# Loading w_in in 2 KB runs from the second chunk on, in a fused attention and feed-forward kernel

## The chip, the cores and the metric

The kernel runs on one core of a Trainium2 chip. The metric is device time in microseconds (us), from one launch to its end; where several runs are given, the median counts. The engines are named as the profile names them: PE is the matrix engine (PEld its weight loads), DVE the vector engine, ACT the scalar engine, POOL the GpSimd engine, and SP the engine that issues most of the transfers (DMA).

## The reference

```
# q, k, v: (8 batches, 8 heads, 576, 64) float32
kv  = einsum('bhsd,bhse->bhde', k, v)
out = einsum('bhsd,bhde->bhse', q, kv)
rms = sqrt(mean(out*out, axis=-1) + 1e-6)
x   = (out / rms * g_norm) -> reshaped to (4608 tokens, 512)

h = x @ w_in               # w_in:  512 x 2048
g = maximum(0.01*h, h)
y = g @ w_out              # w_out: 2048 x 512, y float32
```

The set-up scales the two weight matrices by a float64 number, so they reach the kernel as 8-byte floats and the kernel rounds them to 4-byte floats itself. One row of w_in is 2048 x 8 B = 16 KB, so 128 neighbouring columns of one row are a run of 1 KB, and 256 are a run of 2 KB.

## The kernel before

The 4608 tokens go through in 9 blocks of 512. The first block's feed-forward is done with plain products while the weights are still arriving; the later blocks use a Strassen scheme (seven products in place of eight), in the third and later blocks nested once more for the first product. Only the first block meets the weight loads, so the parts below are those.

w_in is held as four chunks `c`, each of two halves `h` (left and right half of the 2048 columns), each of two parts `u` of 128 columns. A part has four slices `e` of 128 rows.

```python
P, NE, U, NC = 128, 4, 2, 4
NW = U * NE * P
# all of w_in in one tile; per chunk and half the order is part, slice, column
w1_sb = [[view(w1_all, (2 * c + h) * NW, U, NE, P) for c in range(NC)] for h in range(2)]
w2_sb = [[consts.tile([P, U, DM], F32, ...) for c in range(NC)] for h in range(2)]

# seven landing places of 4 KB per partition, used in turn
raw_homes = itertools.cycle([view(stage, i * NW, NW) for i in range(3)]
                            + [pair(i, NW) for i in range(4)])

def load(t, src, eng):          # w_in: 4 transfers, of 32 partitions each; w_out: 1 transfer
    ...
def round_f64(dst, raw):
    lo, hi = raw[:, :, 0], raw[:, :, 1]
    add = spare(...);  pin(nc.scalar.activation(add, lo, func=AF.Copy, scale=2.0 ** -29))
    cut = spare(...);  pin(nc.scalar.activation(cut, hi, func=AF.Copy, scale=2.0 ** -112))
    yield
    pin(nc.vector.tensor_scalar(cut, cut, HIGH_MOST, -HIGH_MOST, ...))       # L246
    yield
    pin(nc.vector.tensor_scalar(dst, cut, 3, None, op0=logical_shift_left))  # L250
    yield
    pin(nc.vector.scalar_tensor_tensor(dst, in0=cut, ..., in1=dst, ...))     # L252
    yield
    pin(nc.vector.tensor_tensor(dst, dst, add, op=ALU.add))                  # L255

w_in_e = w_in.rearrange("(p t i) f -> p i t f", p=NP, i=E)
w_jobs = []
for c in range(NC):
    for h in range(2):
        for u in range(U):
            f0 = h * (DF // 2) + (c * U + u) * P
            w_jobs += [(w1_sb[h][c][:, u], w_in_e[:, :, :, f0:f0 + P]),
                       (w2_sb[h][c][:, u:u + 1, :], w_out[f0:f0 + P].unsqueeze(1))]
w_jobs[1:-1] = [...]     # neighbours swapped: w_in 0, w_in 1, w_out 0, w_in 2, w_out 1, ...
```

There are so 32 jobs of 512 KB, 16 of w_in and 16 of w_out, each a load and a rounding (two operations of ACT, four of DVE). Jobs 0 to 6 are loaded during the attention of the first batch. The first block's loop then runs over the 16 parts n; `between` loads and rounds more jobs ahead of need:

```python
for n in range(2 * NC * U + 1):
    if n < 2 * NC * U:
        c, h, u = n // (2 * U), n // U % 2, n % U
        for e in range(NE):       # product "h_ps" of part n, needs w_in part n
            matmul(h_ps[:, cols], lhsT=w1_sb[h][c][:, u, e, :], rhs=x[:, e, cols], ...)
        act = nc.scalar.activation(gT, h_ps, func=AF.Prelu, alpha=SLOPE)
    ...
    for t in range(4):            # product "o_acc" of part n - 1, needs w_out part n - 1
        matmul(accs[t], lhsT=now[0][:, t * P:(t + 1) * P], rhs=now[1], ...)
    between(n, 1)

def between(n, half):             # cut
    while half and rounded < min(3 * n + 8, 2 * n + 13, len(w_jobs) - (n < 11)):
        if loaded < len(w_jobs):
            load_w(loaded); loaded += 1
            if loaded in (15, 19):
                load_pair(1, (loaded - 15) // 4)     # k, v, q of the second batch
        round_w(rounded); rounded += 1
```

After the first block, w_in in SBUF is read by additions (`sides_w1` on POOL, `combine` on POOL and DVE) and by transfers to a DRAM copy that later blocks read back; all of these index it as `[:, u, e, column]`.

Of the kernel before, what the change touches and what calls it, by code (L numbers as in the profile page):

```python
# [23 lines left out]
def kernel(  # L24
# [38 lines left out]
    DM, DF = w_in.shape  # L63
    P = 128
    NE = DM // P
# [7 lines left out]
    U = 2  # L73
    NC = DF // 2 // (U * P)
# [24 lines left out]
    NW = U * NE * P  # L99
    w1_all = consts.tile([P, 2 * NC * NW], F32, name="w1_all")  # L100
# [4 lines left out]
    def view(t, lo, *shape):  # L105
        n = 1
        for d in shape:
            n *= d
        t = t[:, lo:lo + n]
        names = "abcd"[:len(shape)]  # L110
        return t.rearrange(f"p ({' '.join(names)}) -> p {' '.join(names)}",
                           **dict(zip(names, shape))) if len(shape) > 1 else t
# [83 lines left out]

    w1_sb = [[view(w1_all, (2 * c + h) * NW, U, NE, P) for c in range(NC)] for h in range(2)]
    w2_sb = [[consts.tile([P, U, DM], F32, name=f"w2_{h}_{c}") for c in range(NC)]  # L200
             for h in range(2)]

# [53 lines left out]

    w_in_e = w_in.rearrange("(p t i) f -> p i t f", p=NP, i=E)
    w_jobs = []
    for c in range(NC):
        for h in range(2):  # L260
            for u in range(U):
                f0 = h * (DF // 2) + (c * U + u) * P
                w_jobs += [(w1_sb[h][c][:, u], w_in_e[:, :, :, f0:f0 + P]),
                           (w2_sb[h][c][:, u:u + 1, :], w_out[f0:f0 + P].unsqueeze(1))]

    w_jobs[1:-1] = [w_jobs[i + 1 if i % 2 else i - 1] for i in range(1, len(w_jobs) - 1)]
    w_raws = {}

    def load_w(j, *eng):
# [700 lines left out]
    x_sides, _, sums, _ = sides_x(1)  # L970
# [128 lines left out]
```

## Time and profile before

| | before |
|---|---|
| device time, median of 3 runs | 927.6 us (926.85 to 929.41) |
| span of the profiled run | 925.5 us |
| PE busy | 915.1 us, 99% of the span |
| DVE, ACT, POOL busy | 615.5, 328.7, 317.6 us |
| DMA packets, bytes | 90066, 200.03 MB |

The profile gives the busy time of each engine, then a strip of the span in 40 equal slices, then the transfers, then the chain of work that ended last, then the groups of instructions. A busy PE is the product itself; an idle time is listed under the engine that waited, with what it waited for. A group row ends with how long the engine stood idle ahead of the group and what released it. Two rows of the page say how long an operation of DVE takes on a contiguous tile and on one with a stride between its four rows of 128 elements (`g` is laid out so):

```profile
L610 DVE TENSOR_TENSOR o<-o_c,o 128x512 f32<-128x512 f32 x104 | 71.6, 688 | 117.8 <-PE o_c L118 117.6
...
L610 DVE TENSOR_TENSOR g<-g,pairs 128x512 f32<-128x512 f32 x84 | 55.6, 689 | 1.9
```

### The profile page before, as it was taken

Reading aid. Unit: us, or ns where it says so; the run is one execution under the profiler, and the core shown is the slowest. Engines: PE = TensorE matmul, PEld = TensorE weight load, DVE = VectorE, ACT = ScalarE, POOL = GpSimd, SP = SyncE. Lnnn points to the kernel's source line nnn. Section 1 sums busy time; section 2 is a strip of 40 time slices with the busy share of each in tenths; the row PEclk is TensorE's granted clock in tenths of the full one; section 3 lists DMA queues with packets and bytes.
Section 4 is the critical chain, followed back from the end, with each engine's and each line's share of the span. In section 5 each row is a group of like instructions: output and inputs, shape, how many; then the busy total and the mean of one; then the engine's idle time right before and its main releaser. Section 6 shows DMA issues by size and latency. Waiting matters only on the chain.

```text
span 925.5 us, 17566 instructions
## 1 busy us (share of the span) xinstructions
PE 915.1 (99%) x6856; PEld 776.5 (84%) x6856; DVE 615.5 (67%) x998; ACT 328.7 (36%) x651; POOL 317.6 (34%) x318
## 2 busy tenths in 40 slices
PE   8999999999999999999999999999999999999998
PEld 5544447888998999899999999999988999999996
DVE  4866995587456876597757875687558744654454
ACT  4544532242135233532343423342333333223330
POOL 2000354967622542236211711272225322532222
PEclk9999999999999999999999999999999999999999
DMA  9999936895598678856995599668755676667632
GB/s 270 223 234 217 238 114 193 276 301 165 150 348 266 185 208 297 274 174 189 280 297 181 173 282 276 219 183 229 252 174 175 197 220 186 185 196 220 187 121 91
DMA packets 90066, 200.03 MB, mean 216 GB/s; under 512 B 9856, under 2 KB 42112, under 8 KB 89984
## 3 DMA queue, kind: packets, MB, share of 16 engines
q1 hardware_dynamic: 79392, 186.85, 68.9%
q10 hardware_dynamic: 10144, 10.88, 3.4%
q8 instruction: 55, 0.90, 0.4%
q0 software_dynamic: 448, 1.18, 0.3%
q14 instruction: 27, 0.22, 0.1%
HBM read 172.39 MB, written 26.48 MB: 215 GB/s over the span
## 4 chain that ended last, share of the span: by engine, by line
PE 95%; DMA 2%; DVE 2%; issue 0%; ACT 0%; POOL 0%; SPq 0%; ACTq 0%; DVEq 0%; POOLq 0%
PE o_a L118 21%; PE o_c L118 21%; PE h_ha L118 11%; PE h_hb L118 8%; PE h_hc L118 8%; PE h_hd L118 6%; PE o_acc L118 6%; PE h_ps L118 6%; PE o_ps L118 2%; PE kv_ps L118 2%; PE h_a L118 1%; PE h_b L118 1%; DMA pairs<-in_v_dram 1%; PE h_c L118 1%; PE h_d L118 1%; DMA pairs<-in_moe_w_in_dram 1%
## 5 line engine op out<-in xcount | busy, mean ns | idle before, releaser
L610 POOL TENSOR_TENSOR gs<-g 128x512 f32<-128x512 f32 x64 | 80.8, 1282 | 442.3 <-ACT g L781 442.3
L610 DVE TENSOR_TENSOR o<-o_c,o 128x512 f32<-128x512 f32 x104 | 71.6, 688 | 117.8 <-PE o_c L118 117.6
L781 ACT ACTIVATE g<-g 128x512 f32<-128x512 f32 x124 | 78.2, 631 | 123.4 <-DVE g L610 123.4
L845 ACT COPY w_all<-h_ha 128x512 f32<-128x512 f32 x84 | 48.7, 580 | 186.6 <-PE h_ha L118 186.6
L610 DVE TENSOR_TENSOR o<-o_a,o 128x512 f32<-128x512 f32 x88 | 60.4, 687 | 63.4 <-PE o_a L118 63.3
L118 PE MATMUL o_c<-pairs,gs 128*128 128x256 f32 x384 | 91.3, 381 | 0.0
L118 PE MATMUL o_a<-pairs,gs 128*128 128x256 f32 x384 | 90.8, 379 | 0.0
L118 PEld LDWEIGHTS o_c<-pairs,gs 128*128 128x128 f32 x384 | 69.8, 190 | 9.3 <-issue 1.4
L118 PEld LDWEIGHTS o_a<-pairs,gs 128*128 128x128 f32 x384 | 69.8, 190 | 7.8
L118 PE MATMUL o_c<-w,g 128*128 128x256 f32 x256 | 61.6, 383 | 0.0
L118 PE MATMUL o_a<-w,g 128*128 128x256 f32 x256 | 61.5, 383 | 0.0
L118 PEld LDWEIGHTS h_ha<-stage,w_all 128*128 128x128 f32 x448 | 58.7, 192 | 2.8
L118 PE MATMUL h_ha<-stage,w_all 128*128 128x128 f32 x448 | 59.0, 275 | 0.0
L118 PE MATMUL h_ps<-xT,w_all 128*128 128x512 f32 (+1 forms) x136 | 57.9, 570 | 0.2 <-DVE w_all L255 0.2
L118 PE MATMUL o_acc<-w,g 128*128 128x512 f32 x128 | 57.8, 595 | 0.0
L610 DVE TENSOR_TENSOR g<-g,pairs 128x512 f32<-128x512 f32 x84 | 55.6, 689 | 1.9
L118 PEld LDWEIGHTS o_a<-w,g 128*128 128x128 f32 x256 | 46.4, 190 | 11.0 <-ACT pairs L845 3.1
L610 POOL TENSOR_TENSOR pairs<-w_all 128x512 f32<-128x512 f32 x8 | 11.5, 1438 | 123.5 <-DMA stage<-in_moe_w_in_dram 95.1
L118 PEld LDWEIGHTS o_c<-w,g 128*128 128x128 f32 x256 | 46.4, 190 | 5.8
L118 PEld LDWEIGHTS h_ps<-xT,w_all 128*128 128x128 f32 x136 | 25.5, 190 | 29.2 <-issue 26.5
L118 PEld LDWEIGHTS o_acc<-w,g 128*128 128x128 f32 x128 | 24.0, 190 | 29.8 <-issue 29.4
L610 DVE TENSOR_TENSOR w_all<-h_hc,w_all 128x512 f32<-128x512 f32 x56 | 38.4, 686 | 15.6 <-PE h_hc L118 15.4
(196 smaller groups left out, 2028.0 us busy)
## 6 DMA issues: line engine op xcount, KB each, us to landing
w_all<-w SPq DMA_DIRECT2D x196, 448.0 KB, 4.3
pairs<-w SPq DMA_DIRECT2D x56, 512.0 KB, 4.5
out_dram<-o ACTq DMA_DIRECT2D x36, 256.0 KB, 4.5
v_in<-in_v_dram SPq DMA_DIRECT2D x29, 288.0 KB, 5.7
k_in<-in_k_dram SPq DMA_DIRECT2D x28, 288.0 KB, 6.3
q_in<-in_q_dram SPq DMA_DIRECT2D x56, 144.0 KB, 6.6
q_in<-in_q_dram SPq DMA_DIRECT2D x56, 140.0 KB, 6.6
w<-stage SPq DMA_DIRECT2D x12, 512.0 KB, 4.6
```

The costliest lines, as they stand in the source:

```text
L118: pin(nc.tensor.matmul(*args, **kw))
L610: ins = eng.tensor_tensor(out_, a, b_, op=ALU.subtract if minus else ALU.add)
L781: nc.scalar.activation(t, t if src is None else src, func=AF.Prelu, alpha=SLOPE)
L845: nc.scalar.copy(q[:, at], banks[tag])
```

## The change

From the second chunk on, a job of w_in no longer is one part of 128 columns with all four slices. It is half of the slices (two) for both parts together, 256 neighbouring columns, so that each run in DRAM is 2 KB long where it was 1 KB. It is meant to let the transfers of w_in run with half as many, longer pieces. To make room for that, the order in SBUF becomes slice, part, column; and since both jobs of a half chunk are now needed for either of its parts, the list of jobs is sorted anew: both w_in jobs of a half chunk stand at the place of the first, and the w_out jobs follow. The first chunk keeps its jobs and its order of jobs, but its destination in SBUF gets a stride (four rows of 128, with 256 between their starts).

```diff
-    w1_sb = [[view(w1_all, (2 * c + h) * NW, U, NE, P) for c in range(NC)] for h in range(2)]
+    w1_sb = [[view(w1_all, (2 * c + h) * NW, NE, U, P).rearrange("p e u m -> p u e m")
+              for c in range(NC)] for h in range(2)]
 ...
-    for c in range(NC):
-        for h in range(2):
-            for u in range(U):
-                f0 = h * (DF // 2) + (c * U + u) * P
-                w_jobs += [(w1_sb[h][c][:, u], w_in_e[:, :, :, f0:f0 + P]),
-                           (w2_sb[h][c][:, u:u + 1, :], w_out[f0:f0 + P].unsqueeze(1))]
-
-    w_jobs[1:-1] = [w_jobs[i + 1 if i % 2 else i - 1] for i in range(1, len(w_jobs) - 1)]
+    for n in range(2 * NC * U):
+        c, h, u = n // (2 * U), n // U % 2, n % U
+        f0 = h * (DF // 2) + (c * U + u) * P
+        if c == 0:
+            w1 = w1_sb[h][c][:, u], w_in_e[:, :, :, f0:f0 + P]
+        else:
+
+            f0, e0 = f0 - u * P, u * NE // 2
+            w1 = (view(w1_all, (2 * c + h) * NW + u * NW // 2, NE // 2, U * P),
+                  w_in_e[:, :, e0:e0 + NE // 2, f0:f0 + U * P])
+        w2 = w2_sb[h][c][:, u:u + 1, :], w_out[f0 + u * P * (c > 0):][:P].unsqueeze(1)
+
+        w_jobs += [(n - (u if c else 0), 0, w1), (n + 1, 1, w2)]
+    w_jobs = [job for _, _, job in sorted(w_jobs, key=lambda job: job[:2])]
```

## The prediction

> **What bounds the kernel now.** I read the page's busy times first, then PE's waits, then the stretch in which the weights arrive, and last the instructions around the closest deadlines.
>
> ```profile
> PE 915.1 (99%) x6856; PEld 776.5 (84%) x6856; DVE 615.5 (67%) x998; ACT 328.7 (36%) x651; POOL 317.6 (34%) x318
> ...
> DMA  9999936895598678856995599668755676667632
> ```
>
> PE is busy 99% of the span. The DMA strip is full in slices 1 to 5 (0 to 116 us), where all of w_in and w_out is loaded. So two things look full at once in the first eighth of the run, and the question is which of them PE's end hangs on. The list of PE's waits answers that:
>
> ```profile
> PE o_ps L118 <- issue: 1.7, 1, 1.7
> PE idle_ps L118 <- DVE group L291: 1.5, 1, 1.5
> PE inv_ps L118 <- DVE roots L563: 0.8, 2, 0.4
> PE sum_ps L118 <- ACT flat L550: 0.6, 1, 0.6
> PE o_ps L118 <- DVE kv L321: 0.5, 1, 0.5
> PE h_b L118 <- ACT g L806: 0.4, 1, 0.4
> PE kv_ps L118 <- DMA pairs<-in_v_dram: 0.4, 1, 0.4
> PE h_ps L118 <- DVE w_all L255: 0.2, 1, 0.2
> ```
>
> Columns: who waited, for whom, total us, times, longest. Only the last row has to do with weights: 0.2 us, once, when part 1 of the first chunk was not yet rounded. No later product waited for a weight at all. The stretch of the loads, beside a later stretch whose transfers are mostly long packets (columns: window, length, busy time of each engine, PE clock, DMA share, GB/s):
>
> ```profile
> 27.00:110.00 83.00, 82.83 (x382) 38.44 (x382) 64.57 (x123) 39.92 (x77) 4.52 (x3) 1.00 1.02 228
> ...
> 250.00:275.00 25.00, 25.00 (x234) 23.37 (x233) 14.46 (x24) 7.53 (x14) 5.01 (x4) 1.00 1.04 348
> ```
>
> From 27 to 110 us PE is busy 82.83 of 83.00 us; the missing 0.17 is that one wait. The DMA engines are full there at 228 GB/s, and full at 348 GB/s in the other window, so the loads do run inefficiently; but they run ahead of PE. One job shows how far (timelines of SP, ACT, DVE and PE; job 13, part 7 of w_in, in the kernel before):
>
> ```profile
> 38.15 3.71 SPq L220 DMA_DIRECT2D pairs<-in_moe_w_in_dram  x4
> ...
> 62.85 0.66 ACT L242 ACTIVATE add<-pairs 128x512 uint32<-128x512 uint32 x1
> ...
> 65.74 0.69 DVE L255 CUSTOM_DVE_ANT_0 w_all<-w_all,add 128x1024 uint16<-128x1024 uint16 x1
> ...
> 69.03 3.60 PE L118 MATMUL o_acc<-w,g 128*128 128x512 f32 x8
> ```
>
> It is issued by 41.9 us, landed some 7 us later (the median from issue to landing in the page is 6.5 to 7.3 us for w_in), and ACT reads it at 62.85: about 14 us of waiting in the landing place. ACT waited for a w_in transfer once in the whole run, 2.8 us, for job 0. The pace of the roundings is set by ACT's order of work behind PE's own products, not by the transfers.
>
> **What the Trainium skill says.** (1) Perfetto Trace Analysis, section DMA Optimizations: "Small DMAs (< 2KB) have significant per-transfer overhead." The trace agrees as far as it goes: 228 GB/s against 348 GB/s at the same full share. (2) The same page, Optimization Strategy: look for the gaps on the most contended engine, and for what blocks it there. Here the gaps of PE after 27 us sum to 0.6 us. (3) VectorE: DVE Perf Modes, What auto-detection actually checks: a single-source operation keeps its double rate if the outermost dimensions of source and destination are even. The first chunk's strided destination, 4 rows of 128, is even, so L250 should stay at its 0.43 us; no run here shows that yet. (4) SBUF — State Buffer, SBUF: two separate sides: DVE and POOL hold a shared port in turn. The trace agrees: L250 takes 0.43 us alone, but 1.37 us at 105.01 us, beside a POOL addition that began at 104.54.
>
> **The change part by part.**
>
> Transfers: 12 of 16 w_in jobs (chunks 1 to 3) change from 512 packets of 1 KB to 256 of 2 KB. Packets fall by 12 x 256 = 3072, from 90066 to 86994; bytes stay at 200.03 MB. The 12 jobs are 12 x 0.524 = 6.3 MB. If all of it moved at 348 in place of 228 GB/s, DMA time would fall by 6.3/0.228 - 6.3/0.348 = 27.6 - 18.1 = 9.5 us at most, spread over 27 to 110 us. All of this lies beside PE, which waits for none of it: 0 on the path.
>
> Order of jobs: PE's order of instructions is the same in both programs, and so is POOL's. What moves is which job stands at which place on SP, ACT and DVE. Two things come later: a half chunk's second w_in job is now needed by its first part, and the w_out job between goes back one place. I took the end of the rounding at each place from DVE's timeline of the kernel before (a place does 0.42 + 0.43 + 0.69 + 0.69 us of work whatever the job) and set it against the start of the product that needs it in the new order:
>
> - part 4 needs place 8: 46.21 against 51.86, slack 5.65 us
> - w_out 3, place 9: 52.15 against 55.29, slack 3.14
> - part 6, place 12: 61.81 against 65.59, slack 3.78
> - w_out 5, place 13: 66.43 against 69.03, slack 2.60
> - part 8, place 16: 75.56 against 80.73, slack 5.17
> - w_out 9, place 21: 95.33 against 99.48, slack 4.15
> - all others 6 us or more.
>
> All are positive. In the new program ACT moreover takes some roundings ahead of an activation they used to follow (places 10, 11, 13, 25 to 31), which uses its idle time and makes these slacks larger. Such an ACT operation could hold back the activation behind it if its transfer were late; with about 14 us in hand and faster transfers I give that 0. On the path: 0.
>
> Stride in the first chunk: L250, L252 and L255 of the four w_in jobs write 4 rows of 128. A DVE addition over a tile laid out so takes 689 ns against 688 for a contiguous one, so the cost should be 0 to 0.05 us per instruction (my choice). It is on the path only for job 1, just ahead of the one weight wait. The chain of waits there (start, length, what):
>
> ```profile
> 28.20 0.35 DVE cut L246
> ...
> 28.58 0.44 DVE w_all L250
> ...
> 29.04 0.70 DVE w_all L252
> ...
> 29.76 0.70 DVE w_all L255
> ...
> 30.60 3.67 PE h_ps L118 x8
> ```
>
> Three instructions, so +0 to +0.15 us. PE's weight loads still read 128 contiguous columns: 0. The additions that later read w_in with the new stride already wrote rows of 128, and took 1.26 us like those over contiguous g: 0.
>
> After the first block: the landing places come free earlier (by ACT's new order the last job is read before 116 us rather than at 122.5), so POOL's first additions for w_in can start some 7 us sooner than 123.81. PE did not wait for them before. This shifts which DVE operations meet POOL at the shared port, and could move the 0.45 us wait of h_b at 161.25: -0.4 to +1 us.
>
> Sum: 0 + 0 + (0 to 0.15) + (-0.4 to +1.0), centre +0.1 us, which is a tenth of a thousandth of the time. I predict 927.6 us.
>
> **The rivals.** First, that the loads do pace the first block, in a way that PE's waits hide. For it: the full DMA share from 0 to 116 us. Against it: PE is 82.83 of 83.00 us busy there. If I were wrong and the 9.5 us came off the path, the time would be about 918 us, still inside 2%. Second, that the reordering uses up the slack: one rounding late by more than 2.6 us stalls PE, and the in-order queues could repeat it for each of six half chunks. For it: among the places of chunks 1 to 3 the smallest slack falls from 6.1 us (place 11: 59.48 against 65.59) to 2.60. Against it: DVE has idle time in this stretch (64.57 of 83 us busy). If each half chunk lost 1 us, the time would be 933 to 934 us. Third, that the strided destination loses the double rate of L250 (0.43 to about 0.69 us, the time of L252, which runs at the single rate): +0.27 us at job 1 and perhaps as much at job 0, +0.5 us in all, 928.1 us.
>
> **Range and chances.** PE's own work is unchanged, so the time can fall by no more than about 0.6 us of waits after 27 us plus whatever the start gives, and rise only through new waits. The three runs of before span 926.85 to 929.41 us, which is wider than my sum. Range 926.2 to 929.6 us. Faster by over 2% would need 18.5 us, more than all of PE's 10.4 us of idle time (925.5 - 915.1): 1%. Slower by over 2% needs 18.5 us of new stalls: 1%. Within 2%: 98%.
>
> **What would show it.** Right: 86994 packets; PE's waits after 27 us still below 1.5 us with no row of several w_all or w entries; a higher rate or a lower DMA share between 27 and 110 us; about 14 us or more between the landing and the reading of a w_in job; L250 still at 0.43 us. Wrong: waits of h_ps or o_acc for DVE w_all or w (second rival), PE's stretch from 27 to 144 us shorter (first rival), L250 of the first chunk at 0.6 us or more (third rival).

## The result, and the profile after

| | before | after |
|---|---|---|
| device time, median of 4 runs each, us | 928.5 (926.85 to 929.84) | 936.26 (934.82 to 936.87) |
| ratio, 95% interval | | 1.0082 (1.006 to 1.0104) |
| span of the profiled run, us | 925.5 | 933.1 |
| DMA share at GB/s, 27 to 100 us | 1.01 at 225 | 0.86 at 224 |

The change makes the kernel 0.8% slower: within the 2% that was called likely, but outside the range of 926.2 to 929.6 us. The packets fell as the change intends. Here are the strip of the DMA engines and the count of packets from the page of the kernel after:

```profile
DMA  9897753976399568855896588658756666667632
DMA packets 86994, 200.03 MB, mean 214 GB/s; under 512 B 9856, under 2 KB 35968, under 8 KB 86912
```

The packets are the predicted 86994. The share of the DMA engines in the window from 27 to 100 us falls from 1.01 to 0.86 at the same rate, which looks like what the longer pieces were meant to do; the experiments below do not bear that out. PE did not wait for the transfers before and gains nothing. What is new stands in PE's waits (who waited, for whom, total us, times, longest):

```profile
PE h_ps L118 <- DVE w_all L256: 3.1, 1, 3.1
...
PE o_ps L118 <- DVE kv L328: 1.4, 2, 0.9
...
PE o_ps L118 <- DVE qT L432: 0.2, 1, 0.2
```

(The lines of the rounding moved down by one, so L251, L253 and L256 after are L250, L252 and L255 before; those behind the list of jobs moved down by 7. In the experiments they differ again by a few lines. Of the 1.4 us, 0.5 is the wait before the first block that the kernel before has too.) So there are two new losses, at two places.

**Start of the first block.** PE's timeline before, then PE's and DVE's after (start, us, what, wait ahead of it in brackets), and two windows of the kernel after (window, length, busy of PE, PEld, DVE, ACT and POOL, PE clock with 1.00 as full speed, DMA share, GB/s). Each product shows as two instructions.

```profile
26.71 3.72 PE L118 MATMUL h_ps<-xT,w_all 128*128 128x256 f32 x16
...
34.11 3.60 PE L118 MATMUL o_acc<-w,g 128*128 128x512 f32 x8
```

```profile
26.41 0.70 PE L118 MATMUL h_ps<-xT,w_all 128*128 128x256 f32 x2
30.21 8.41 PE L118 MATMUL h_ps<-xT,w_all 128*128 128x256 f32 x22 [3.10 <-DVE w_all L256]
38.45 3.60 PE L118 MATMUL o_acc<-w,g 128*128 128x512 f32 x8
...
28.27 0.43 DVE L251 TENSOR_SCALAR w_all<-cut 128x512 uint32<-128x512 uint32 x1
28.74 0.69 DVE L253 SCALAR_TENSOR_TENSOR w_all<-cut,w_all 128x512 uint32<-128x512 uint32 x1
29.46 0.69 DVE L256 CUSTOM_DVE_ANT_0 w_all<-w_all,add 128x1024 uint16<-128x1024 uint16 x1
```

```profile
30.00:33.00 3.00, 2.79 (x7) 2.25 (x8) 2.86 (x7) 0.23 (x1) 0.00 (x0) 0.55 1.04 219
33.00:36.00 3.00, 3.00 (x12) 2.22 (x11) 2.86 (x6) 0.60 (x1) 0.00 (x0) 0.89 1.00 337
```

Part 0 does its first product, of slice 0, and then stops until L256 has finished job 1 (30.15 us; PE goes on at 30.21). But job 1 is part 1; part 0 needs only job 0. After the wait, PE's clock is 0.55 in one window of 3 us and 0.89 in the next. From the start of part 0 to the first o_acc it now takes 12.04 us; before it took 7.40 us (26.71 to 34.11). That is +4.64 us.

**The attention of the second batch, at 111 us.** The timelines of ACT, DVE, POOL and PE, first before, then after:

```profile
99.68 0.60 ACT L926 ACTIVATE g<-h_ps 128x512 f32<-128x512 f32 x1 [3.30 <-PE h_ps L118]
100.74 0.68 ACT L244 ACTIVATE cut<-pairs 128x512 f32<-128x512 f32 x1
...
103.10 0.47 DVE L321 COPY kv<-kv_ps 128x128 f32<-128x128 f32 x2
...
101.50 1.73 POOL L610 TENSOR_TENSOR pairs<-w_all 128x512 f32<-128x512 f32 x1 [95.12 <-DMA stage<-in_moe_w_in_dram]
...
102.91 3.60 PE L118 MATMUL h_ps<-xT,w_all 128*128 128x512 f32 x8
106.44 0.98 PE L118 MATMUL o_ps<-qT,kv 64*32 64x448 f32 x16
107.35 3.70 PE L118 MATMUL o_acc<-w,g 128*128 128x512 f32 x8
```

```profile
101.35 0.70 ACT L245 ACTIVATE cut<-pairs 128x512 f32<-128x512 f32 x1
...
104.00 0.60 ACT L933 ACTIVATE g<-h_ps 128x512 f32<-128x512 f32 x1 [0.58 <-PE h_ps L118]
...
102.46 1.39 DVE L251 TENSOR_SCALAR w_all<-cut 128x512 uint32<-128x512 uint32 x1
103.89 1.64 DVE L253 SCALAR_TENSOR_TENSOR w_all<-cut,w_all 128x512 uint32<-128x512 uint32 x1
105.56 1.64 DVE L256 CUSTOM_DVE_ANT_0 w_all<-w_all,add 128x1024 uint16<-128x1024 uint16 x1
...
108.76 1.67 DVE L256 CUSTOM_DVE_ANT_0 w_all<-w_all,add 128x1024 uint16<-128x1024 uint16 x1
...
111.44 0.47 DVE L328 COPY kv<-kv_ps 128x128 f32<-128x128 f32 x2
...
102.14 1.43 POOL L617 TENSOR_TENSOR pairs<-w_all 128x512 f32<-128x512 f32 x1 [95.77 <-DMA stage<-in_moe_w_in_dram]
...
107.23 3.60 PE L118 MATMUL h_ps<-xT,w_all 128*128 128x512 f32 x8
111.77 1.16 PE L118 MATMUL o_ps<-qT,kv 64*32 64x448 f32 x12 [0.94 <-DVE kv L328]
...
113.99 3.70 PE L118 MATMUL o_acc<-w,g 128*128 128x512 f32 x8
```

Read it relative to PE. The h_ps before this attention starts at 102.91 before and at 107.23 after. POOL's first addition begins 1.41 us ahead of it before, and 5.09 us ahead of it after. What it waits for, I infer, is ACT's last reading of a job in a landing place, since the additions write `pairs`, where four of the landing places are. It begins 0.08 us after such a reading ends before (101.42) and 0.09 us after one ends after (102.05), though the profile names a transfer that had landed long ago; in four experiments the distance is 0.08 to 0.09 us too. Before, ACT reads this job behind an activation of PE's result (99.68); after, ahead of one (104.00). So POOL's additions now meet two roundings that DVE has still to do before the copy kv; four of their operations take 1.39, 1.64, 1.64 and 1.67 us where they take 0.43, 0.69, 0.69 and 0.69 alone: +3.84 us. The copy moves from 0.19 us behind the start of h_ps to 4.21 us behind it, 4.0 us later, and it had some 2.9 us in hand (its end at 103.57 against o_ps at 106.44). From this h_ps to the o_acc behind the attention it takes 6.76 us in place of 4.44: +2.32 us, of which 0.94 + 0.19 us are listed as waits. The rest lies mostly in o_ps, which falls into two pieces of 1.16 and 0.94 us where it took 0.98; why each piece takes so long was not followed up.

Sum: the profiled run of after begins the block 0.30 us sooner, loses 4.64 and 2.32, loses another 0.17 by the last product, and takes 0.77 us longer from there to the end: 7.6 us, which is 933.1 - 925.5. The last two terms were not followed up.

### The profile page after: what moved, and what is told of

Its sections match the earlier page's. It is cut to its first block, busy times and chain, and to the rows that moved or that the text cites. A ratio compares the mean times of both kernels' runs of the same rounds, so it can differ in the third digit from the quotient of the medians.

```text
span 933.1 us, 17568 instructions
## 1 busy us (share of the span) xinstructions
PE 918.9 (98%) x6856; PEld 778.2 (83%) x6856; DVE 617.2 (66%) x998; ACT 329.3 (35%) x651; POOL 317.2 (34%) x318
## 2 busy tenths in 40 slices
DMA packets 86994, 200.03 MB, mean 214 GB/s; under 512 B 9856, under 2 KB 35968, under 8 KB 86912
## 3 DMA queue, kind: packets, MB, share of 16 engines
q10 hardware_dynamic: 10144, 10.88, 3.4%
## 4 chain that ended last, share of the span: by engine, by line
PE 91%; DMA 4%; DVE 3%; ACT 1%; SPq 0%; issue 0%; ACTq 0%; DVEq 0%
PE o_a L118 21%; PE o_c L118 21%; PE h_ha L118 11%; PE h_hb L118 8%; PE h_hc L118 8%; PE h_hd L118 6%; PE h_ps L118 4%; PE o_acc L118 4%; PE o_ps L118 2%; PE kv_ps L118 2%; PE h_a L118 1%; PE h_b L118 1%; DMA pairs<-in_moe_w_in_dram 1%; DMA stage<-in_moe_w_in_dram 1%; PE h_c L118 1%; PE h_d L118 1%
## 5 line engine op out<-in xcount | busy, mean ns | idle before, releaser
L118 PE MATMUL h_ps<-xT,w_all 128*128 128x512 f32 (+1 forms) x136 | 59.8, 585 | 3.1 <-DVE w_all L256 3.1
```

Source lines behind the costliest of these rows:

```text
L118: pin(nc.tensor.matmul(*args, **kw))
```

## The experiments

The start of part 0 in the trace lies between 26.3 and 30.1 us from one profiled execution to the next. That goes mostly with one wait of o_ps in the first batch, of 0.2 to 3.5 us. So besides the device time I give the length from the start of part 0 to the start of the last group of PE's products, against 892.76 us before (26.71 to 919.47); after it is 899.89, +7.13. All ratios are device time to the kernel before on the same chip. They differ a little from the ratios of the medians, which are for the kernel before 928.77 us beside the first four experiments and 929.07 us beside the other four; the difference is largest for the kernel with job 3 in the gaps, 1.0092 against 939.86 / 929.07 = 1.0116, which still lies inside its interval.

My theory after the traces: the new wait at the start comes from the layout of the first chunk, the wait at 111 us from the order of the jobs, and the 2 KB transfers cost nothing. Rivals: the transfers in 2 KB runs come late somewhere, or one of the two waits causes the other.

**The change, with the first chunk in its old layout.**

```diff
 view(w1_all, (2 * c + h) * NW, NE, U, P).rearrange("p e u m -> p u e m")
+    if c else view(w1_all, (2 * c + h) * NW, U, NE, P)
```

> The change with the first chunk of w_in left in its old order in SBUF (part, slice, column, no gaps); 2 KB loads and the sorted list of jobs stay. Theory: the change lost 4.1 us at the start because the products of part 0, from slice 1 on, wait for the rounding of part 1, whose destination with gaps spans theirs (3.1 us of wait and about 1.3 us of slower PE clock), and 2.3 us at 111 us because the sorted list lets POOL begin earlier beside DVE. Then only the second loss stays: about 930.8 us, no wait of h_ps for DVE above 0.5 us at the start, the wait of o_ps for the kv copy still there. Rival 'the 2 KB loads do it': about 935 us. Rival 'the second loss follows from the first': about 928.5 us and no wait of o_ps.

Measured: 932.29 us, ratio 1.0028 (1.0011 to 1.0045); length +3.23 us. The wait at the start is back at 0.2 us and part 0 to o_acc takes 7.39 us. The wait at the attention stays (0.96 and 0.19 us, stretch of 6.77 us). The loss at the start, 4.1 us in the expectation, is 4.64 us by the lines above. So the first loss needs the layout of the first chunk, and the second does not follow from the first. Of the length, 2.33 us lie in that stretch; 0.7 us of the other 0.9 come after the first block and are not explained.

**The kernel before, with only the first chunk's new layout.**

```diff
-view(w1_all, (2 * c + h) * NW, U, NE, P)
+view(w1_all, (2 * c + h) * NW, NE, U, P).rearrange("p e u m -> p u e m")
+    if c == 0 else view(w1_all, (2 * c + h) * NW, U, NE, P)
```

> The kernel before with nothing but the new order in SBUF (slice, part, column) for the first chunk; loads of 1 KB and the old list of jobs. Theory: the first loss alone, a wait of h_ps for DVE of about 3 us before slice 1 of part 0, a PE clock below 1 right after it, and about 932.6 us. Rival 'the 2 KB loads do it': 928.5 us. Rival 'the second loss follows from the first': about 935 us, with a wait of o_ps for the kv copy.

Measured: 934.48 us, ratio 1.0062 (1.0046 to 1.0078); length +7.15 us. PE's timeline of this kernel:

```profile
26.77 0.70 PE L118 MATMUL h_ps<-xT,w_all 128*128 128x256 f32 x2
30.57 9.54 PE L118 MATMUL h_ps<-xT,w_all 128*128 128x256 f32 x22 [3.10 <-DVE w_all L257]
39.95 2.31 PE L118 MATMUL o_acc<-w,g 128*128 128x512 f32 x5
```

It is the same wait, with no 2 KB transfer and no new order. Part 0 to o_acc takes 13.18 us, +5.78. The wait at the attention isn't there. So the layout of the first chunk alone makes the first loss. The other 1.4 us of its length come later; 0.7 of them is one wait for a transfer (h_ha for w_all), which I did not follow up.

**The kernel before, with only the new order of jobs (1 KB runs, old layout).**

```diff
-w_jobs[1:-1] = [...]                      # neighbours swapped
+w_jobs += [(n - (u if c else 0), 0, w1), (n + 1, 1, w2)]     # w1, w2 as before
+w_jobs = [job for _, _, job in sorted(w_jobs, key=lambda job: job[:2])]
```

> The kernel before with nothing but the sorted list of jobs; layout and loads of 1 KB as before. Theory: the second loss alone: POOL begins about 4 us earlier against PE than in the kernel before, DVE's roundings beside it take 1.4 to 1.7 us in place of 0.4 to 0.7, o_ps waits for the kv copy, about 930.8 us. Both rivals: 928.5 us and no such wait.

Measured: 931.91 us, ratio 1.0032 (1.0007 to 1.0056); length +2.47 us. Its timelines show the same collision:

```profile
101.06 1.39 DVE L250 TENSOR_SCALAR w_all<-cut 128x512 uint32<-128x512 uint32 x1
...
110.38 1.16 PE L118 MATMUL o_ps<-qT,kv 64*32 64x448 f32 x12 [0.93 <-DVE kv L320]
```

POOL begins at 100.73, 5.12 us ahead of the h_ps before the attention, and the stretch takes 6.75 us. The order alone makes the second loss. In these three experiments the times lie 1.1 to 1.9 us above what I expected, while the waits are those expected.

**2 KB runs, with the first chunk's old layout and the old order of jobs.**

```diff
-w_jobs += [(n - (u if c else 0), 0, w1), (n + 1, 1, w2)]
+w_jobs += [(n, 0, w1), (n + 1, 1, w2)]    # and the layout as in the first experiment
```

> The change with the first chunk of w_in in its old order in SBUF and the old list of jobs; only the 2 KB loads of chunks 1 to 3 (and their layout) are left. Theory: both losses gone, 928.5 us within 1 us; a wait of at most 0.5 us before part 4, whose second half now stands at place 9. Rival 'the 2 KB loads do it': about 935 us. Rival 'the second loss follows from the first': 928.5 us.

Measured: 929.7 us, ratio 1.0002 (0.9985 to 1.0019); length -0.17 us. It has the 86994 packets of the change and neither of its waits. POOL begins at

```profile
103.61 1.28 POOL L618 TENSOR_TENSOR pairs<-w_all 128x512 f32<-128x512 f32 x1 [97.23 <-DMA stage<-in_moe_w_in_dram]
```

which is 1.41 us ahead of its h_ps (105.02), as before, and the stretch takes 4.44 us. The transfers alone change the time by nothing that can be told from 0: the interval is -0.15% to +0.19%.

Nor do they explain the DMA share. Here are the windows from 27 to 100 us of the order alone, with runs of 1 KB, and of the 2 KB runs alone:

```profile
27.00:100.00 73.00, 71.86 (x375) 34.53 (x376) 52.22 (x104) 37.33 (x74) 0.00 (x0) 1.00 0.88 228
27.00:100.00 73.00, 72.41 (x377) 34.92 (x378) 53.57 (x106) 36.22 (x71) 0.00 (x0) 1.00 0.99 234
```

The order of jobs alone brings the share to 0.88, near the 0.86 of the change; the 2 KB runs alone leave it at 0.99. The rate divided by the share says the same. It is 236 GB/s with the 2 KB runs alone, inside the 223 to 239 of the four kernels with 1 KB runs and the old order (before, and three of these experiments); with the new order it is 245 to 267, and 259 of that with 1 KB runs. Each figure is one execution. So no trace here shows that the longer pieces move the bytes at less cost. What the order does to the share is open.

**Is the wait at the start a wait for what lies in the gaps?** In the kernel before, the gaps of the first chunk's left half are given to the other half, so that job 3, rounded later than job 1, fills them:

```diff
+view(w1_all, 2 * c * NW, U, NE, 2, P)[:, :, :, h, :] if c == 0
+    else view(w1_all, (2 * c + h) * NW, U, NE, P)
```

> The kernel before, the first chunk of w_in again laid out with gaps of 128 columns, but the gaps of part 0 are now filled by part 2 (the same part of the other half), whose rounding is two places later (job 3 instead of job 1). Theory (a product that reads inside the gaps of a later-needed rounding waits for that rounding): h_ps waits until the rounding of job 3 ends, 2 x 2.25 us later than with the change, so 7.6 us of wait instead of 3.1, and with the slower clock after it about 938 us. Rival 'a destination or an operand with gaps is slow in itself': the same 3.1 us as with the change, about 934 us.

Measured: 939.86 us, ratio 1.0092 (1.0055 to 1.0129); length +9.97 us.

```profile
35.07 0.69 DVE L256 CUSTOM_DVE_ANT_0 w_all<-w_all,add 128x1024 uint16<-128x1024 uint16 x1
...
35.82 9.40 PE L118 MATMUL h_ps<-xT,w_all 128*128 128x256 f32 x22 [7.60 <-DVE w_all L256]
```

Part 0 still needs only job 0, but waits until its new neighbour, job 3, is rounded (35.76 us). If the stride as such, the rounding of job 0 or the reading of a strided operand were the cause, it would have stayed at 3.1 us.

**How much of the loss is the wait, and how much the clock after it?** The second experiment with seven products of zeros in the gap, which add nothing to the result:

```diff
+if n == 0 and part == 0 and e == 0:
+    for _ in range(7):
+        matmul(h_ps[:, N2:], lhsT=zeros[:, :P], rhs=zeros[:, :N2], ...)
```

> The run with only the first chunk's new layout, with 7 products of zeros put into PE's wait before slice 1 of part 0 (they add zero to the other half of the accumulator). Theory: the wait for the rounding stays 3.1 us, but PE is busy in it, so the clock stays at 1.00 and the 2 to 3 us that the products lose after the wait come back: about 932 us. Rival 'the 9.5 us that the products after the wait take have another cause, such as more waits on roundings': no change, about 934.5 us.

Measured: 932.49 us, ratio 1.0031 (1.0018 to 1.0043). PE's timeline:

```profile
30.61 3.19 PE L118 MATMUL h_ps<-g 128*128 128x256 f32 x14
33.88 6.72 PE L118 MATMUL h_ps<-xT,w_all 128*128 128x256 f32 x22
```

The 22 instructions behind the gap take 6.72 us, where they took 9.54 in the second experiment and 8.41 in the change. Part 0 to o_acc takes 10.36 us, 2.82 less than without the zeros: that is the clock. The other 2.96 us (10.36 - 7.40) are close to the wait, 3.10 - 0.17 = 2.93 us. The same sum fits the change, 2.93 + (8.41 - 6.72) = 4.62 of 4.64 us, and the kernel with job 3 in the gaps, 7.43 + (9.40 - 6.72) = 10.11 of 10.13.

**Is the loss at the attention POOL's early start?** The first experiment's kernel, with a copy of three elements on POOL that must follow the copy kv, ahead of its additions:

```diff
+nc.gpsimd.tensor_copy(view(pairs, NW, 3, NW)[:, :, :1], kvs[1][:, 0, :3].unsqueeze(2))
```

> The change with the first chunk in its old layout (2 KB loads and sorted list kept), plus one POOL copy of three elements that reads the kv copy and writes the tile that POOL's first additions fill, so POOL begins only after DVE has made the kv copy. Theory: the roundings before the kv copy take 0.4 to 0.7 us again, o_ps does not wait, the remaining 2.6 us go: 928.5 to 929 us. Rival 'ACT reading its jobs ahead of the activation is what delays o_ps, not POOL': about 931 us, the wait of o_ps for kv stays.

Measured: 934.37 us, ratio 1.005 (1.0036 to 1.0064); length +4.96 us. The expectation of the time missed. Its timelines:

```profile
142.01 1.12 ACT L934 ACTIVATE g<-h_ps 128x512 f32<-128x512 f32 x2
...
106.41 0.19 POOL L981 COPY pairs<-kv 128x3 f32<-128x3 f32 x1 [99.99 <-DVE kv L329]
...
142.70 7.68 PE L118 MATMUL o_acc<-w,g 128*128 128x512 f32 x14 [2.99 <-ACT g L934]
```

The wait at the attention is gone with the early start, as the theory says: the order of jobs is the new one and o_ps no longer waits for kv. What comes in its place is a second wait that the new order had prepared. With the old order, DVE begins to reduce for the normalization of the second batch (rms) 16.1 us behind the h_ps ahead of the attention; with the sorted list, alone or in the change, it does so 28.3 us behind it. ACT waits for that normalization (10.88 us here, until 136.70), and the activations of PE's results come behind it. In the first experiment the one that matters ends 0.13 us before o_acc begins, and PE just does not wait:

```profile
139.40 0.63 ACT L934 ACTIVATE g<-h_ps 128x512 f32<-128x512 f32 x1
...
140.16 7.07 PE L118 MATMUL o_acc<-w,g 128*128 128x512 f32 x16
```

With the small copy PE gets there 2.2 us earlier, measured from that h_ps, and ACT's activation starts 0.9 us later (36.38 in place of 35.49 us). So PE waits 2.99 us and then runs at a clock of 0.57 from 143 to 146 us. The order of jobs thus takes the slack at two places, and the wait at the attention had hidden the other. A kernel in which the early additions are left out altogether was not tried.

**How much room have the transfers?** The kernel before, with w_in from job 7 on in runs of 512 B, by cutting each load in two by columns:

```diff
-load(to, src, eng)
+for i in range(cuts):                     # cuts = 2 for w_in from job 7 on
+    load(to[..., i * m:(i + 1) * m], src[..., i * m:(i + 1) * m], eng)
```

> The kernel before with every w_in job from the seventh on loaded in runs of 512 B, twice as many packets as before, same list, same layout. Theory (the loads lie beside PE and land well before ACT reads them): within 1 us of before, 928.5 us, DMA share higher or the loads later, but no wait of PE for a rounding. Rival 'the loads pace the first block': slower by several us, with ACT waiting for w_in transfers.

Measured: 932.44 us, ratio 1.0031 (1.0014 to 1.0047); length +4.22 us. It missed in part: no product waits for a weight longer than the 0.2 us of before, but one waits for v of the second batch:

```profile
93.67 2.19 PE L118 MATMUL kv_ps<-v_in,k_in 64*64 64x64 f32 x70 [2.60 <-DMA v_in<-in_v_dram]
```

The wait of 2.60 us and the slower clock behind it (0.51 from 94 to 97 us) make up most of the 4.22. SP issues the loads in order, and issues this v at 86.65 in place of 82.70 us. So the weights have room, and the loads of k and v behind them in the queue have less. The rival, ACT waiting for several transfers of w_in, did not appear: it waits for one, job 0, as before.

No version here beats the kernel before: its PE is busy 99% of the span, and the version that keeps the 2 KB runs without the two waits equals it.

## Why the prediction was wrong

*Transfers: 0 on the path.* Right: the packets are as counted, and the version with the transfers alone has ratio 1.0002. The first rival, loads that pace the block, falls with it. But the "9.5 us at most" of DMA time was drawn from two windows of the kernel before (228 and 348 GB/s) as if the length of the pieces made the difference, and no run bears that out. The lower DMA share, which I had named as a sign of being right, came by luck: the order alone gives 0.88 with 1 KB runs, the 2 KB runs alone 0.99.

*Stride in the first chunk.* The third rival falls: L251 of job 1 takes 0.43 us on the strided destination and L253 and L256 0.69, so the cost of the operations is 0 as said. The step that failed is the sentence "PE's weight loads still read 128 contiguous columns: 0". The columns read are the same; the dependence is not. Part 1 of the first chunk now occupies columns 128 to 1023 of the half chunk with gaps of 128, and part 0's slices 1 to 3 lie in those gaps. The program makes part 0 wait for the rounding of part 1, and the kernel with job 3 in the gaps shows that it waits for whoever fills them (3.1 us, then 7.6 us). I looked at what each instruction costs and at which data a product needs, and did not look at which semaphore the product waits for in the changed program. In place of "+0 to +0.15 us" the term is +4.64 us in the change and +5.78 alone: 2.93 of wait and 1.7 to 2.8 of clock.

On the clock, the Trainium skill (TensorE: Matmul & The Clock Gate, What's actually happening) says that PE's clock is halved after an idle window of about 3.4 us and comes back after as long a stretch of work. The runs agree in kind: 0.55 in the three microseconds after a wait of 3.10 us, 1.00 when the wait was filled with products. But waits of 2.44 to 3.10 us were enough, shorter than the window it gives.

*Order of jobs: "On the path: 0".* The slacks of the weights held: no o_acc waits for w, and h_ps waits for w_all only in part 0. The second rival, as I described it (a rounding late for its own product), did not occur. What the step left out is a product that needs no weight: o_ps of the second batch needs kv and qT, which DVE makes in order behind two roundings. I wrote that ACT's taking roundings ahead of an activation "makes these slacks larger"; it also frees a landing place earlier, which lets POOL start. And it left out the normalization of the second batch, which the new order puts 12 us later on DVE; the change itself shows no wait there, but the kernel that holds POOL back does.

*POOL's first additions.* I gave the shift at the shared port -0.4 to +1 us and looked for it at h_b, with POOL's additions moving away from 123.81. The mechanism was right; place and size were wrong. h_b kept its 0.4 us. POOL's first additions begin at 101.50; I had used one of them (104.54) as an example of the shared port and not as a thing that could move. They move 3.7 us ahead relative to PE, into two roundings that stand before the copy kv, and the term is +2.32 us (+2.31 with the order alone). The skill (SBUF — State Buffer, SBUF: two separate sides) has the port held for a whole instruction by one of the two; four operations that each take 0.95 to 0.98 us longer beside additions of 1.3 to 1.7 us fit that.

*The range.* It was drawn around a sum in which all terms were 0 or noise. My own list of what would show it wrong contained waits of h_ps for w_all, and this is what came, for another reason than the one I gave.

## What to carry to other kernels

When a change interleaves two destinations in one tile, ask of every reader what it waits for in the changed program, since a reader that lies in another writer's gaps can wait for that writer (here 3.1 us, and 7.6 us with a later neighbour), though no operation got slower. When a list of jobs is reordered, check not only the consumers of the jobs but everything that stands behind them on the same engine, and which engine is set free earlier and what it then collides with. Before a lower DMA share is put down to longer transfers, run the transfers alone. And a short wait of PE costs more than its length: here another 1.7 to 2.8 us of slower clock for 3.1 us.

## What the runs showed of the hardware

PE's clock fell after every wait of 2.44 us or more, and after none of 1.89 us or less: 0.51 in the window of 94 to 97 us behind the wait of 2.60 us for v, 0.57 in 143 to 146 us behind the 2.99 us for ACT, 0.50 in 30 to 36 us behind the 3.10 us of the second experiment; behind the 0.94 and 0.19 us at the attention it stayed at 1.00 (111 to 115 us of the kernel after). The attention of the first batch brings the two closest cases. Here are o_ps of the first experiment and of the 2 KB runs alone, each with the window from 19 to 22 us behind its wait:

```profile
18.59 1.49 PE L118 MATMUL o_ps<-qT,kv 64*32 64x256 f32 x37 [1.89 <-issue]
19.00:22.00 3.00, 2.94 (x47) 1.36 (x25) 2.07 (x6) 2.08 (x5) 0.00 (x0) 1.00 1.13 210
18.80 2.77 PE L118 MATMUL o_ps<-qT,kv 64*32 64x256 f32 x37 [2.44 <-issue]
19.00:22.00 3.00, 3.00 (x41) 1.28 (x30) 1.45 (x4) 1.46 (x3) 0.00 (x0) 0.54 1.17 201
```

The same 37 instructions take 1.49 us at a clock of 1.00 and 2.77 us at the lower one. Where between 1.89 and 2.44 us the limit lies, or whether it is the same each time, no run shows. After the wait of 7.60 us the 22 instructions took 9.40 us, no longer than the 9.54 us after 3.10: the loss of clock did not grow with the wait. Seven products of zeros in the gap kept the clock at 1.00. And whether transfers of 2 KB load the DMA engines less than those of 1 KB, these runs do not show.
